# Moving the rows of x and b to every second and every fourth partition in an FFT, expert and GLU kernel

## Chip, cores and metric

The kernel runs on one core of one Trainium2 chip. The metric is the device time of one execution in microseconds (us).

## What is computed

Three layers run one after the other over 8 batches of 3072 tokens of 256 channels. Weights and inputs are random float32.

```
X = np.fft.rfft(x, axis=1)
Y = X * (filt_r + 1j * filt_i)[None, :, :]
y = np.fft.irfft(Y, n=3072, axis=1)              # layer 1: a filter along the sequence
x = y.reshape(B * S, D)
skip = x @ w_skip; e = argmax(x @ w_gate)         # layer 2: one of 8 experts for tokens with skip > 0
x += gate * (relu(x @ w1[e]) @ w2[e])             #          (only for those tokens)
xn = x / rms(x) * rms_g                           # layer 3: a gated linear unit
out = (silu(xn @ w_gate) * (xn @ w_val)) @ w_out
```

## The kernel before

`fft_route` (L159) does layer 1 and the choice of experts. A sequence of 3072 tokens is seen as 96 rows of 32 tokens (N1 = 96, N2 = 32). A product with a 96x96 matrix goes over the 96 rows (stage 1), one with 24 matrices of 128x128 over the 32 columns (stage 2), the filter is applied, the same goes back (stage 3), and a 96x96 product ends it (stage 4). Between the stages the data must change its layout, and that is done through DRAM:

| transfer | line | SBUF partitions | size, transfers per step |
|---|---|---|---|
| x, input to SBUF | L209 | 96 | 384 KB, 2 |
| a_d, stage 1 to DRAM | L404 | 96 | 384 KB, 2 |
| a, DRAM to stage 2 | L370 | 128 | 768 KB, 1 |
| b_d, stage 3 to DRAM | L455 | 128 | 768 KB, 1 |
| b, DRAM to stage 4 | L379 | 96 | 768 KB, 1 |
| y, stage 4 to DRAM | L477 | 96 | 384 KB, 2 |

The work is cut into 32 steps, a quarter (Q = 4) of a batch each. The loop at L655 runs as a pipeline by hand: in step s stage 1 works on quarter s, stages 2 and 3 on quarter s - 5, stage 4 on quarter s - 10, and the routing on quarter s - 11. After step 31 nothing is left for stage 1, and the pipeline drains until step 45. The list `seq` (L677) is the order in which the pieces of a step are written down: `f` is stage 2, `v` stage 3 (its third piece, `vp`, is done at the start of the next step), `u1` stage 1, `u4` stage 4, `qu` the squares of x on ScalarE, `tr`, `logits`, `choose`, `rank`, `place`, `gate` and `sc` the routing. Every engine runs its instructions in that order.

All of these transfers are issued from SyncE (SP). Its queue is in order: a transfer whose semaphore isn't there yet holds back all that stand behind it. The transfers take eight semaphores in turn, so each one also waits until the eighth before it has landed.

- `load_x` (L203) fetches x two steps ahead into six tiles of half a step.
- `load_a2` (L364) stands at the very start of step s and fetches the tile for step s + 1. It reads whole columns, so the first of a batch (s divisible by 4) needs all of stage 1's writes of that batch. The last of these is issued at the end of step s - 1.
- `load_b4` (L374) stands behind `vp` and fetches the tile for stage 4 of step s + 1. The first of a batch (s = 9, 13, 17, ...) needs all four of stage 3's writes of that batch. The last of these is issued by `vp`, right ahead of it.
- Stage 1's matmul (L395) takes its x tile, stage 4's (L471) its b tile, as the moving operand, with the 96x96 constants `d1` and `d4`.

When the pipeline drains, the generator `then` (`moe`, L903) takes the room of the x tiles (`front`) for expert weights and tokens. `glu` (L1523) is the last layer.

Of the kernel before, what the change touches and what calls it, by code (L numbers as in the profile page):

```python
# [10 lines left out]
F32 = mybir.dt.float32  # L11
F16 = mybir.dt.float16
I32 = mybir.dt.int32
U32 = mybir.dt.uint32
ACTF = mybir.ActivationFunctionType
# [5 lines left out]
NB, S, D = 8, 3072, 256  # L21
N1, N2, NG = 96, 32, 24
# [19 lines left out]
def shape_constants():  # L42


    pi2 = 2.0 * np.pi
    n1 = np.arange(N1)
    d1 = np.zeros((N1, 4, NG))
    d4 = np.zeros((4, NG, N1))
    t2 = np.zeros((NG, 4, N2, 2, 2, N2))
    t3 = np.zeros((NG, 2, 2, N2, 4, N2))  # L50
    sgn = np.zeros((2, 2, N2, NG))
    kk = np.zeros((2, 2, N2, NG), np.int64)
    n2 = np.arange(N2)
    k2 = np.arange(N2)
    for g in range(NG):
        for u in range(2):
            q = 2 * g + u
            if q == 0:
                for ri, k1 in ((0, 0), (1, N1 // 2)):
                    d1[:, ri, g] = np.cos(pi2 * n1 * k1 / N1)  # L60
                    d4[ri, g, :] = np.cos(pi2 * n1 * k1 / N1) / S
                k = np.where(k2 < 16, N1 * k2, N1 // 2 + N1 * (k2 - 16))
                th = pi2 * np.outer(n2, k) / S
                for s in range(N2):
                    ri = 0 if s < 16 else 1
                    t2[g, ri, :, 0, u, s] = np.cos(th[:, s])
                    t2[g, ri, :, 1, u, s] = -np.sin(th[:, s])
                    t3[g, 0, u, s, ri, :] = 2 * np.cos(th[:, s])
                    t3[g, 1, u, s, ri, :] = -2 * np.sin(th[:, s])
                t2[g, 0, :, 1, u, 0] = np.cos(np.pi * n2)  # L70
                t3[g, 0, u, 0, 0, :] = 1.0
                t3[g, 1, u, 0, 0, :] = np.cos(np.pi * n2)
                kk[0, u, :, g] = k
                kk[1, u, :, g] = k
                kk[1, u, 0, g] = S // 2
                sgn[0, u, :, g] = -1.0
                sgn[1, u, :, g] = 1.0
                sgn[:, u, 0, g] = 0.0
            else:
                d1[:, 2 * u, g] = np.cos(pi2 * n1 * q / N1)  # L80
                d1[:, 2 * u + 1, g] = -np.sin(pi2 * n1 * q / N1)
                d4[2 * u, g, :] = 2 * np.cos(pi2 * n1 * q / N1) / S
                d4[2 * u + 1, g, :] = -2 * np.sin(pi2 * n1 * q / N1) / S
                k = q + N1 * k2
                th = pi2 * np.outer(n2, k) / S
                t2[g, 2 * u, :, 0, u, :] = np.cos(th)
                t2[g, 2 * u + 1, :, 0, u, :] = np.sin(th)
                t2[g, 2 * u, :, 1, u, :] = -np.sin(th)
                t2[g, 2 * u + 1, :, 1, u, :] = np.cos(th)
                t3[g, 0, u, :, 2 * u, :] = np.cos(th).T  # L90
                t3[g, 1, u, :, 2 * u, :] = -np.sin(th).T
                t3[g, 0, u, :, 2 * u + 1, :] = np.sin(th).T
                t3[g, 1, u, :, 2 * u + 1, :] = np.cos(th).T
                up = k > S // 2
                kk[:, u, :, g] = np.where(up, S - k, k)
                sgn[0, u, :, g] = np.where(up, 1.0, -1.0)
                sgn[1, u, :, g] = np.where(up, -1.0, 1.0)
    f = np.float32

    p = np.arange(128)[:, None]  # L100
    w = np.arange(NB * 24)[None, :]
    n, t = np.divmod(w % 6 * 128 + p, N1)
    tok = w // 24 * S + N2 * t + w // 6 % 4 * 8 + n
    return {
        "c_d1": d1.transpose(0, 2, 1).reshape(N1, N1).astype(f),
        "c_d4": d4.transpose(1, 0, 2).reshape(N1, N1).astype(f),
        "c_t2": t2.reshape(NG, 128, 128).transpose(1, 0, 2).astype(f),
        "c_t3": t3[0].reshape(128, 128).astype(f),
        "c_sgn": sgn.reshape(2, 64, NG).transpose(1, 0, 2).reshape(64, 2 * NG).astype(f),
        "c_tri": (np.arange(128)[:, None] < np.arange(128)[None, :]).astype(np.float16),  # L110
        "c_tok": np.stack([tok, 0 * tok], axis=2).astype(np.int32).reshape(128, 2 * NB * 24),
        "c_pri": np.broadcast_to((NE - np.arange(NE)).astype(f), (128, 6, NE)),
        "c_blk": np.concatenate([
            CAP * np.arange(NE), np.zeros(2 * NE),
            (np.arange(NE)[None, :] < np.arange(NE)[:, None]).ravel(), np.arange(NBLK + 8),
        ]).astype(f)[None, :],
        "c_cap": np.broadcast_to((CAP * np.arange(NE)).astype(f), (128, NE)),
    }, kk.reshape(128, NG)
# [40 lines left out]
def fft_route(tc, x, filr, fili, w9, consts, y_dram, lst, lp, front, shared, then):  # L159
# [13 lines left out]
    with ExitStack() as ctx:  # L173
# [2 lines left out]
            tc.tile_pool(name=name, bufs=bufs, **kw))  # L176
        dp = pool("f_dram", 1, space=DRAM)
        cp = pool("f_const", 1, side="right")
        b4p = pool("f_b4", 2, side="right")
        yp = pool("f_y", 4, side="right")  # L180
        tp = pool("f_t", 2, side="right")
        rp = pool("f_r", 2, side="right")
# [15 lines left out]
            (eng or nc.sync).dma_start(out=t, in_=src)  # L198
            return t

        x_t = {}

        def load_x(s):  # L203
            if s < steps:
                b, q = divmod(s, Q)
                for h in range(2):
                    t = front.tile([N1, HC, D], F32, tag="x", name="x")
                    n = q * CH + h * HC
                    nc.sync.dma_start(  # L209
                        out=t, in_=x[b].rearrange("(p n) c -> p n c", p=N1)[:, n:n + HC, :]  # L210
                    )
                    x_t[s, h] = t

        d1 = const("d1", [N1, N1], F32, consts["c_d1"])
        load_x(0)
        load_x(1)
        t2 = fp.tile([128, NG, 128], F32, name="t2")
# [42 lines left out]
                axis=AX.X, op=ALU.max, apply_absolute_value=True,  # L260
            )

        d4 = cp.tile([N1, N1], F32, name="d4")
        tri = cp.tile([128, 128], F16, name="tri")
        pri = cp.tile([128, RC, NE], F32, name="pri")
        basee = lp.tile([128, NE], F32, name="basee")
# [107 lines left out]
        def load_b4(s):  # L374
            if not 0 <= s < steps:
                return
            b, q = divmod(s, Q)
            t = b4p.tile([N1, CH, D], F32, tag="b4", name="b4")
            nc.sync.dma_start(out=t, in_=b_d[b % 3][:, q * CH:(q + 1) * CH])  # L379
            b4_t[s] = t  # L380

        def stage1(s):

            b, q = divmod(s, Q)
            if q == 0:
                sq_t[b] = rp.tile([N1, 2 * Q], F32, tag="sq", name="sq", bufs=4)
            at = {}

            def part(i):
                h, o = divmod(2 * i, HC)  # L390
                xt = x_t[s, h]
                if o == 0:
                    at[h] = ap.tile([N1, HC, D], F32, tag="a", name="a")
                ps = ps_d.tile([N1, 2 * D], F32, tag="d", name="ps1")
                nc.tensor.matmul(  # L395
                    out=ps, lhsT=d1, rhs=xt[:, o:o + 2, :].rearrange("p n c -> p (n c)"),
                    start=True, stop=True,
                )
                nc.scalar.copy(
                    out=at[h][:, o:o + 2, :].rearrange("p n c -> p (n c)"), in_=ps  # L400
                )
                if o + 2 == HC:
                    n = q * CH + h * HC
                    nc.sync.dma_start(out=a_d[b % 3][:, n:n + HC, :], in_=at[h])  # L404

            def square(h):
                jk = fp.tile([N1, HC, D], F16, tag="jk", name="jk")
                nc.scalar.activation(
                    out=jk, in_=x_t[s, h], func=ACTF.Square,
                    accum_out=sq_t[b][:, 2 * q + h:2 * q + h + 1],  # L410
                )
            return [lambda i=i: part(i) for i in range(CH // 2)], [
# [241 lines left out]
        vp = []  # L654
        for s in range(steps + lagr + 3):  # L655
            s2, s4, sr = s - lag2, s - lag4, s - lagr
            load_a2(s2 + 1)
            if s < Q - 1:
                load_x(s + 2)
            for fn in startup.get(s, []):  # L660
# [4 lines left out]
            if s % Q == 2 and lagr < s < steps + Q:  # L665
# [9 lines left out]

            r1a, r1b = ({}, r1) if steps + 5 < s <= steps + 10 else (r1, {})
            seq = [  # L677
                f[0:1], sc[0:1], vp, [lambda: load_b4(s4 + 1)], fmx[0:1], u1[0:1],
                g(r1, "logits"), [lambda: load_x(s + 2)] if s >= Q - 1 else [], qu[0:1], f[1:2],
                tr[0:1], u1[1:2], g(r1, "choose"), sc[1:3], u4[0:1], v[0:1], fmx[1:2], f[2:3],  # L680
                tr[1:2], u4[1:2], g(r1a, "rank"), qu[1:2], g(r1a, "place"), sc[3:5], u1[2:3],
                tr[2:3], v[1:2], fmx[2:3], g(r1, "gate"), u4[2:3], sc[5:6], tr[3:4], u1[3:4],
                u4[3:4], g(r1b, "rank"), g(r1b, "place"), sq,
            ]
            vp = v[2:3]
# [217 lines left out]
def moe(tc, y_dram, lst, c_blk, w1, w2, wsp, lp, front, shared):  # L903
# [12 lines left out]
        while shared["step"] < n:  # L916
            yield

    wf = [front.tile([128, FE], F32, tag="x", name="m_wf") for _ in range(4)]
    x = front.tile([128, 4, D], F32, tag="x", name="m_x")  # L920
    xs = front.tile([128, 4, 2 * D], F16, tag="x", name="m_xs")
    ws = lp.tile([128, 16], F32, name="m_ws")
    ones = lp.tile([128, 128], F32, name="m_ones")

# [788 lines left out]
def run_all(tc, x, filr, fili, w9, w1, w2, wg, wv, wo, rg, consts, out):  # L1713
    with tc.tile_pool(name="scratch", bufs=1, space=DRAM) as dp:
# [1 line left out]
        lst = dp.tile([NE * CAP + TB, 2], I32, name="lst")  # L1716
        wsp = dp.tile([NE, 128, WROW], F16, name="wsp")
        with tc.tile_pool(name="lists", bufs=1, side="right") as lp, ExitStack() as before:
            front = before.enter_context(tc.tile_pool(name="front", bufs=6))
            mctx = tc.manual_schedule()  # L1720
            mctx.__enter__()
            shared = {"ps_m": before.enter_context(tc.tile_pool(name="ps_m", bufs=1, space=PSUM))}
# [41 lines left out]
```

## Time and profile before

| | us |
|---|---|
| median of 3 runs | 3391.66 (3383.09 to 3394.03) |
| profiled execution, its own time | 3414.32 |
| its span, first to last instruction | 3412.5 |
| TensorE busy | 3196.1 |
| VectorE busy | 2255.2 |
| ScalarE busy | 2259.5 |
| GpSimd busy | 1530.4 |

The profile cuts the span into 40 slices of 85 us. The first seven are the FFT, the next nine are mostly the experts, the rest is the GLU. A digit is the busy share of an engine in tenths. The DMA line is the mean busy share of 16 DMA engines, and the one under it what they moved in GB/s. An engine in this kernel waits only for a semaphore: where it idles, the timeline names in brackets how long and what released it.

### The profile page before, as it was taken

How to read it: one execution, taken by the hardware profiler on the slowest of the kernel's cores; microseconds unless marked ns; L12 is line 12 of the kernel's file. 1: busy time of each engine (PE TensorE's matmuls, PEld its weight loads, DVE VectorE, ACT ScalarE, POOL GpSimd, SP SyncE). 2: the span in 40 equal slices, each digit the busy share in tenths (PEclk: the TensorE clock that was granted, in tenths of full speed). 3: DMA queues.
4: the chain of work that ended last, by engine and by line, in shares of the span. 5: the costliest groups of instructions: out<-in, count | busy, mean ns of one | idle time of the engine just before them, and what ended most of it. 6: DMA issues, size and time to landing. Idle time of an engine off the chain costs nothing.

```text
span 3412.5 us, 60927 instructions
## 1 busy us (share of the span) xinstructions
PE 3196.1 (94%) x21784; PEld 2172.4 (64%) x21784; DVE 2255.2 (66%) x4818; ACT 2259.5 (66%) x4950; POOL 1530.4 (45%) x1546
## 2 busy tenths in 40 slices
PE   7888887688998988999999999999999999999999
PEld 3555554355555655767767777776776776776776
DVE  3777776488998645666666666666666666666664
ACT  5556654566766755676676676777667667667665
POOL 2355566456565643344334334334334433433433
PEclk8999997799999999999999999999999999999999
DMA  9899997355556462212111211211221211121110
GB/s 279 276 262 281 275 276 205 109 160 163 166 166 178 132 180 81 56 45 46 51 45 41 56 42 44 55 37 45 47 50 45 47 50 45 44 53 45 41 37 19
DMA packets 374683, 364.73 MB, mean 107 GB/s; under 512 B 260964, under 2 KB 320372, under 8 KB 370022
## 3 DMA queue, kind: packets, MB, share of 16 engines
q1 hardware_dynamic: 357430, 335.28, 35.0%
q0 software_dynamic: 16944, 25.51, 2.6%
q8 instruction: 173, 2.83, 0.3%
q14 instruction: 136, 1.11, 0.1%
HBM read 157.96 MB, written 133.80 MB: 85 GB/s over the span
## 4 chain that ended last, share of the span: by engine, by line
PE 57%; ACT 3%; DVE 1%; DMA 0%; issue 0%; SPq 0%; DVEq 0%; ACTq 0%
PE psa L1581 21%; PE o L1660 20%; PE psb L1581 16%; ACT gc L1598 1%; DVE vc L1592 1%; ACT jk L772 1%; ACT s L1588 0%; ACT hh L1614 0%; DVE rsq_g L132 0%; ACT ot L1673 0%; ACT u L1588 0%; DMA x<-y 0%; PE m_o L1128 0%; DMA xT<-xs 0%; DVE ss L774 0%
## 5 line engine op out<-in xcount | busy, mean ns | idle before, releaser
L1617 POOL TENSOR_TENSOR hl<-vc,hh 128x384 f16<-128x384 f32 x768 | 699.2, 914 | 1247.5 <-ACT hh L1614 1247.1
L1660 PE MATMUL o<-g_wo,hh 128*128 128x256 f16 x4608 | 878.8, 273 | 0.0
L1660 PEld LDWEIGHTS <-hh 128*128 128x128 f16 x4608 | 450.7, 98 | 296.7
L1660 PE MATMUL o<-g_wo,hl 128*128 128x256 f16 x2304 | 628.0, 273 | 0.0
L1581 PE MATMUL psa<-xT,g_vhi 128*128 128x384 f16 x1488 | 484.2, 326 | 8.2 <-DVE vc L1592 8.2
L1581 PE MATMUL psa<-xT,g_ghi 128*128 128x384 f16 x1488 | 484.2, 326 | 0.5 <-DVE gc L1592 0.3
L1614 ACT CAST hh<-vc 128x384 f16<-128x384 f32 x768 | 394.2, 513 | 13.6 <-DVE vc L1604 13.5
L1604 DVE SCALAR_TENSOR_TENSOR vc<-vc,g_st,gc 128x384 f32<-128x384 f32 x576 | 378.8, 680 | 5.7
L1588 ACT COPY s<-psa 128x384 f32<-128x384 f32 x384 | 182.9, 476 | 297.8 <-PE psa L1581 297.7
L1581 PE MATMUL psb<-xT,g_vhi 128*128 128x384 f16 x1116 | 363.1, 326 | 0.0
L1581 PEld LDWEIGHTS <-g_ghi 128*128 128x128 f16 x2688 | 263.0, 98 | 123.2
L1598 ACT ACTIVATE gc<-gc,g_st 128x384 f32<-128x384 f32 x576 | 338.6, 616 | 0.0
L1581 PE MATMUL psb<-xT,g_ghi 128*128 128x384 f16 x1116 | 332.8, 326 | 0.1
L1581 PEld LDWEIGHTS <-g_vhi 128*128 128x128 f16 x2688 | 262.9, 98 | 102.7
L1110 PE MATMUL psa<-m_xT,m_w 128*128 128x512 f16 (+1 forms) x1344 | 318.4, 377 | 9.8 <-DMA m_xT<-m_xs 8.0
L1128 PE MATMUL m_o<-m_w,m_hh 128*128 128x256 f16 x1740 | 305.6, 277 | 14.0 <-PEq L1331 11.1
L1588 ACT COPY s<-psb 128x384 f32<-128x384 f32 x384 | 183.4, 478 | 202.0 <-PE psb L1581 201.8
L1128 PE MATMUL m_o<-m_w,m_hl 128*128 128x256 f16 x870 | 241.4, 277 | 43.2 <-POOL m_hl L1121 32.5
L1581 PE MATMUL psa<-xT,g_glo 128*128 128x384 f16 x744 | 242.5, 326 | 0.0
L1581 PE MATMUL psa<-xT,g_vlo 128*128 128x384 f16 x744 | 242.5, 326 | 0.0
L1660 PEld LDWEIGHTS <-hl 128*128 128x128 f16 x2304 | 225.4, 98 | 26.0 <-POOL hl L1617 0.2
L1592 DVE TENSOR_TENSOR vc<-psb,s 128x384 f32<-128x384 f32 x192 | 106.6, 555 | 196.8 <-PE psb L1581 194.8
(254 smaller groups left out, 6322.6 us busy)
## 6 DMA issues: line engine op xcount, KB each, us to landing
x<-in_x_dram SPq DMA_DIRECT2D x64, 384.0 KB
a_d<-a SPq DMA_DIRECT2D x64, 384.0 KB
a<-a_d SPq DMA_DIRECT2D x32, 768.0 KB
b_d<-bt SPq DMA_DIRECT2D x32, 768.0 KB
b<-b_d SPq DMA_DIRECT2D x32, 768.0 KB
y<-y SPq DMA_DIRECT2D x64, 384.0 KB
x<-y SPq DMA_DIRECT2D x28, 768.0 KB
out_dram<-ot SPq DMA_DIRECT2D x27, 768.0 KB
```

The source lines that it names most:

```text
L772: ops = [(SQUARES[t], lambda t=t: nc.scalar.activation(out=jk, in_=x[:, t, :], func=ACTF.Square, accum_out=ss[:, t:t + 1])) for t in range(T)]
L1110: nc.tensor.matmul(out=ps, lhsT=w[:, k, fs], rhs=d["xT"][:, o + k, 0:n], start=(j == 0), stop=(j == 5),)
L1128: nc.tensor.matmul(out=o[t // 2][:, t % 2, :], lhsT=h[:, ts_], rhs=w_["w2"][:, f, i, :], start=(f == k == t % 2 == 0), stop=(f == KF - 1 a ...
L1581: nc.tensor.matmul(out=ps, lhsT=w_[m][:, q, k, :], rhs=xT[:, o + k, :], start=(j == 0 and bank == p), stop=(j == 2), skip_group_check=True,)
L1588: nc.scalar.copy(out=z[m, n], in_=z[m, p])
L1592: v.tensor_tensor(out=z[m, n], in0=z[m, p], in1=z[m, b], op=ALU.add)
L1598: nc.scalar.activation(out=z["g", n], in_=src, func=ACTF.Silu, scale=st[:, 20:21])
L1604: v.scalar_tensor_tensor(out=z["v", n], in0=src, scalar=st[:, 21:22], in1=z["g", n], op0=ALU.mult, op1=ALU.mult,)
L1614: nc.scalar.copy(out=part(hh, n), in_=z["v", n])
L1617: nc.gpsimd.tensor_tensor(out=part(hl, n), in0=z["v", n], in1=part(hh, n), op=ALU.subtract)
L1660: nc.tensor.matmul(out=o_t[b][:, t % 2, :], lhsT=h[:, f, ts_], rhs=wo16[:, 2 * q + f, k, :], start=(j == 0 and q == 0 and n == first_of[b] ...
```

## The change

Each tile of x and of b now has 128 partitions and holds a whole step (`x_all` has three of them, `b4_all` two). Rows 0 to 63 lie on partitions 0, 2, 4 to 126, and rows 64 to 95 on partitions 1, 5, 9 to 125; `load_rows` needs two transfers for that, of 512 and 256 KB. The other 32 partitions hold zeros, written once by five memsets at the start. `d1` and `d4` are spread in the same way, and the products run over 128 partitions. x keeps two transfers per step, b has two in place of one. A batch's first load of a moves from the start of the step to behind `load_x`, and a batch's first load of b from behind `vp` to behind the second piece of stage 3. Other loads of a and b keep their places.

```diff
+    def spread(d):
+        out = np.zeros((128, N1))
+        out[0::2] = d[0:64]
+        out[1::4] = d[64:]
+        return out.astype(f)
...
-        "c_d1": d1.transpose(0, 2, 1).reshape(N1, N1).astype(f),
-        "c_d4": d4.transpose(1, 0, 2).reshape(N1, N1).astype(f),
+        "c_d1": spread(d1.transpose(0, 2, 1).reshape(N1, N1)),
+        "c_d4": spread(d4.transpose(1, 0, 2).reshape(N1, N1)),
...
+        def load_rows(t, rows):
+            nc.sync.dma_start(out=t[0:128:2], in_=rows[0:64])
+            nc.sync.dma_start(out=t[1:128:4], in_=rows[64:N1])
+
+        x_all = [t.rearrange("p (n c) -> p n c", c=D) for t in front]
...
-                for h in range(2):
-                    t = front.tile([N1, HC, D], F32, tag="x", name="x")
-                    n = q * CH + h * HC
-                    nc.sync.dma_start(
-                        out=t, in_=x[b].rearrange("(p n) c -> p n c", p=N1)[:, n:n + HC, :]
-                    )
-                    x_t[s, h] = t
-
-        d1 = const("d1", [N1, N1], F32, consts["c_d1"])
+                load_rows(x_all[s % 3], x[b].rearrange("(p n) c -> p n c", p=N1)[
+                    :, q * CH:(q + 1) * CH, :])
+
+        b4_all = [b4p.tile([128, CH, D], F32, name=f"b4{i}") for i in range(2)]
+        for i, t in enumerate(front + b4_all):
+            (nc.vector, nc.gpsimd)[i % 2].memset(t, 0.0)
+        d1 = const("d1", [128, N1], F32, consts["c_d1"])
         load_x(0)
         load_x(1)
...
-            t = b4p.tile([N1, CH, D], F32, tag="b4", name="b4")
-            nc.sync.dma_start(out=t, in_=b_d[b % 3][:, q * CH:(q + 1) * CH])
+            t = b4_all[s % 2]
+            load_rows(t, b_d[b % 3][:, q * CH:(q + 1) * CH])
...
-                jk = fp.tile([N1, HC, D], F16, tag="jk", name="jk")
+                jk = fp.tile([128, HC, D], F16, tag="jk", name="jk")
...
-            load_a2(s2 + 1)
+            la, lb = [lambda: load_a2(s2 + 1)], [lambda: load_b4(s4 + 1)]
+            la0, la1 = ([], la) if (s2 + 1) % Q == 0 else (la, [])
+            lb0, lb1 = ([], lb) if (s4 + 1) % Q == 0 else (lb, [])
+            for fn in la0:
+                fn()
...
-                f[0:1], sc[0:1], vp, [lambda: load_b4(s4 + 1)], fmx[0:1], u1[0:1],
-                g(r1, "logits"), [lambda: load_x(s + 2)] if s >= Q - 1 else [], qu[0:1], f[1:2],
+                f[0:1], sc[0:1], vp, lb0, fmx[0:1], u1[0:1],
+                g(r1, "logits"), [lambda: load_x(s + 2)] if s >= Q - 1 else [], la1, qu[0:1], f[1:2],
...
-                tr[2:3], v[1:2], fmx[2:3], g(r1, "gate"), u4[2:3], sc[5:6], tr[3:4], u1[3:4],
+                tr[2:3], v[1:2], lb1, fmx[2:3], g(r1, "gate"), u4[2:3], sc[5:6], tr[3:4], u1[3:4],
...
-    wf = [front.tile([128, FE], F32, tag="x", name="m_wf") for _ in range(4)]
-    x = front.tile([128, 4, D], F32, tag="x", name="m_x")
-    xs = front.tile([128, 4, 2 * D], F16, tag="x", name="m_xs")
+    room = [front[(4 * NB + i) % 3][:, h * FE:(h + 1) * FE] for i in range(3) for h in range(2)]
+    wf = room[0:4]
+    x = room[4].rearrange("p (t c) -> p t c", t=4)
+    xs = room[5].bitcast(F16).rearrange("p (t c) -> p t c", t=4)
```

How the order moves is seen on SP, whose queue the other engines wait for. This is the queue before, in steps 16 and 17 (`a_d_157` is what stage 1 wrote of batch 3, `b_d_162` what stage 3 wrote of batch 2; step 17 begins at the second load of a):

```order
L370 DMA a_1787<-a_d_157 128x6x256
L455 DMA b_d_162<-bt 128x6x256
L379 DMA b_1819<-b_d_161 96x2048
L209 DMA x<-in_x_dram 96x1024 x2
L404 DMA a_d_158<-a 96x1024
L477 DMA y<-y 96x1024
L404 DMA a_d_158<-a 96x1024
L477 DMA y<-y 96x1024
L370 DMA a_1982<-a_d_157 128x6x256
L455 DMA b_d_162<-bt 128x6x256
L379 DMA b_2013<-b_d_162 96x2048
L209 DMA x<-in_x_dram 96x1024 x2
```

The first row waits for the write of a_d that stands just ahead of it, and the load of `b_2013` for the write right over it. This is step 16 of the changed kernel on SP:

```order
L466 DMA b_d_168<-bt 128x6x256
L211 DMA b_119<-b_d_167 64x2048
L212 DMA b_119<-b_d_167 32x2048
L211 DMA x_66<-in_x_dram 64x2048
L212 DMA x_66<-in_x_dram 32x2048
L382 DMA a_1824<-a_d_163 128x6x256
L415 DMA a_d_164<-a 96x1024
L488 DMA y<-y 96x1024
L415 DMA a_d_164<-a 96x1024
L488 DMA y<-y 96x1024
```

The batch's first load of a has moved from the head of the step to behind five other transfers. And this is step 17 of the changed kernel, again on SP:

```order
L382 DMA a_1954<-a_d_163 128x6x256
L466 DMA b_d_168<-bt 128x6x256
L211 DMA x_67<-in_x_dram 64x2048
L212 DMA x_67<-in_x_dram 32x2048
L415 DMA a_d_164<-a 96x1024
L488 DMA y<-y 96x1024
L211 DMA b_118<-b_d_168 64x2048
L212 DMA b_118<-b_d_168 32x2048
L415 DMA a_d_164<-a 96x1024
L488 DMA y<-y 96x1024
```

Four transfers now stand between the write of b_d and the first load that needs it. On TensorE the order of the matmuls is what it was, step by step.

## Rows read from the trace of the kernel before

**Rows 1.** The page's 40 slices of the span: TensorE, DMA share and GB/s.

```profile
PE   7888887688998988999999999999999999999999
...
DMA  9899997355556462212111211211221211121110
GB/s 279 276 262 281 275 276 205 109 160 163 166 166 178 132 180 81 56 45 46 51 45 41 56 42 44 55 37 45 47 50 45 47 50 45 44 53 45 41 37 19
```

**Rows 2.** Windows: us, engines' busy time (instructions), granted clock, DMA share, GB/s.

```profile
core 0: us, PE busy (x) PEld busy (x) DVE busy (x) ACT busy (x) POOL busy (x), PEclk, DMA share, GB/s
159.00:498.00 339.00, 298.07 (x1705) 184.35 (x1701) 243.79 (x643) 202.84 (x404) 189.72 (x177) 0.96 0.93 274
...
1600.00:3412.00 1812.00, 1797.15 (x12975) 1268.72 (x12972) 1147.95 (x2158) 1264.75 (x2880) 720.87 (x773) 1.00 0.18 45
```

**Rows 3.** TensorE's timeline: first logits matmul of steps 13, 18, 19, 20, 32, 34, 35.

```profile
158.70 0.20 PE L545 MATMUL lg<-w9s,yh 128*128 128x18 f16 x2
...
247.10 0.20 PE L545 MATMUL lg<-w9s,yh 128*128 128x18 f16 x2
...
267.40 0.20 PE L545 MATMUL lg<-w9s,yh 128*128 128x18 f16 x2
...
282.27 0.20 PE L545 MATMUL lg<-w9s,yh 128*128 128x18 f16 x2
...
491.30 0.20 PE L545 MATMUL lg<-w9s,yh 128*128 128x18 f16 x2
...
517.43 0.20 PE L545 MATMUL lg<-w9s,yh 128*128 128x18 f16 x2
...
535.48 0.20 PE L545 MATMUL lg<-w9s,yh 128*128 128x18 f16 x2
```

**Rows 4.** SP's waits, 0 to 580 us: line, releaser, us in total, times, longest.

```profile
SPq L379 <- DMA b_d<-bt: 83.0, 8, 13.4
SPq L370 <- DMA a_d<-a: 46.4, 7, 11.7
```

**Rows 5.** SP's timeline, steps 15 to 17: start, us, line, transfer.

```profile
213.42 0.30 SPq L404 DMA_DIRECT2D a_d<-a  x1
...
222.67 0.38 SPq L370 DMA_DIRECT2D a<-a_d  x1
...
234.88 0.38 SPq L455 DMA_DIRECT2D b_d<-bt  x1
247.90 0.32 SPq L379 DMA_DIRECT2D b<-b_d  x1
```

**Rows 6.** TensorE's timeline, step 18: the wait for b.

```profile
253.85 1.07 PE L471 MATMUL ps<-b,d 96*96 96x512 f32 x2 [3.84 <-DMA b<-b_d]
```

**Rows 7.** Windows: step 16's transfers, the pause behind them, and TensorE after b's wait.

```profile
226.00:230.00 4.00, 3.22 (x13) 1.65 (x12) 2.20 (x9) 2.29 (x5) 3.20 (x4) 1.00 1.09 375
230.00:236.00 6.00, 5.38 (x43) 3.19 (x42) 4.73 (x8) 3.58 (x7) 2.74 (x3) 1.00 1.03 250
236.00:240.00 4.00, 4.00 (x26) 2.59 (x25) 3.77 (x12) 2.78 (x6) 2.77 (x3) 1.00 1.11 377
246.00:248.00 2.00, 2.00 (x29) 1.30 (x29) 1.72 (x3) 1.28 (x4) 0.08 (x1) 1.00 0.00 1
...
254.00:258.00 4.00, 4.00 (x11) 2.74 (x11) 0.00 (x0) 1.17 (x2) 0.90 (x1) 0.63 1.02 349
```

**Rows 8.** Windows of the start: x alone (96 partitions); filters fr and fi (64 partitions).

```profile
5.00:11.00 6.00, 5.41 (x8) 1.73 (x8) 0.00 (x0) 3.30 (x7) 0.00 (x0) 1.00 1.03 266
42.00:46.00 4.00, 4.00 (x9) 2.32 (x9) 2.71 (x4) 1.06 (x2) 0.53 (x1) 0.50 1.00 204
```

**Rows 9.** Timeline of the first 6 us: x's transfers and TensorE's first wait.

```profile
1.21 2.97 SPq L209 DMA_DIRECT2D x<-in_x_dram  x6
...
5.59 5.47 PE L395 MATMUL ps<-x,d 96*96 96x512 f32 x8 [5.59 <-DMA x<-in_x_dram]
```

**Rows 10.** Memsets by source and by line: ns or busy us, mean ns.

```profile
L998 POOL MEMSET m_x<- x1: 945/945/945, 514.0 to 514.0; 128x1024 f32 x1
...
L294 DVE MEMSET ones<- 128x128 f32 x1 | 0.2, 165 | 0.8 <-PEq L1753 0.8
```

More of the change, by code (lines that the diff above doesn't have):

```diff
@@ L178, in fft_route @@
         cp = pool("f_const", 1, side="right")
-        b4p = pool("f_b4", 2, side="right")
+        b4p = pool("f_b4", 1, side="right")
         yp = pool("f_y", 4, side="right")
@@ L199, in const @@
             return t
-        x_t = {}
+        def load_rows(t, rows):
+            nc.sync.dma_start(out=t[0:128:2], in_=rows[0:64])
+            nc.sync.dma_start(out=t[1:128:4], in_=rows[64:N1])
+        x_all = [t.rearrange("p (n c) -> p n c", c=D) for t in front]
         def load_x(s):
@@ L261, in filter_max @@
             )
-        d4 = cp.tile([N1, N1], F32, name="d4")
+        d4 = cp.tile([128, N1], F32, name="d4")
         tri = cp.tile([128, 128], F16, name="tri")
@@ L385, in stage1 @@
             if q == 0:
-                sq_t[b] = rp.tile([N1, 2 * Q], F32, tag="sq", name="sq", bufs=4)
+                sq_t[b] = rp.tile([128, 2 * Q], F32, tag="sq", name="sq", bufs=4)
             at = {}
@@ L390, in part @@
                 h, o = divmod(2 * i, HC)
-                xt = x_t[s, h]
                 if o == 0:
@@ L395, in part @@
                 nc.tensor.matmul(
-                    out=ps, lhsT=d1, rhs=xt[:, o:o + 2, :].rearrange("p n c -> p (n c)"),
+                    out=ps, lhsT=d1, rhs=x_all[s % 3][:, 2 * i:2 * i + 2, :].rearrange("p n c -> p (n c)"),
                     start=True, stop=True,
@@ L406, in square @@
             def square(h):
-                jk = fp.tile([N1, HC, D], F16, tag="jk", name="jk")
+                jk = fp.tile([128, HC, D], F16, tag="jk", name="jk")
                 nc.scalar.activation(
-                    out=jk, in_=x_t[s, h], func=ACTF.Square,
+                    out=jk, in_=x_all[s % 3][:, h * HC:(h + 1) * HC, :], func=ACTF.Square,
                     accum_out=sq_t[b][:, 2 * q + h:2 * q + h + 1],
@@ L1718, in run_all @@
         with tc.tile_pool(name="lists", bufs=1, side="right") as lp, ExitStack() as before:
-            front = before.enter_context(tc.tile_pool(name="front", bufs=6))
+            fp = before.enter_context(tc.tile_pool(name="front", bufs=1))
+            front = [fp.tile([128, 8 * D], F32, name=f"x{i}") for i in range(3)]
             mctx = tc.manual_schedule()
```

## The prediction

> **What bounds the kernel now.** I read the 40 slices first [rows 1]. The DMA digit is 9 or 8 in the first six slices, where 262 to 281 GB/s move, and falls to 2 or 1 in the second half, where TensorE shows 9 throughout. The GLU has no room for this change: TensorE is busy for 1797.15 of 1812.00 us there [rows 2]. All that the change touches lies in the FFT, roughly the first 570 us. In its steady part, 159 to 498 us, TensorE is busy for 298.07 of 339.00 us, at a mean granted clock of 0.96, while the DMA engines show a share of 0.93 and 274 GB/s [rows 2]. Two resources are nearly full there, and neither is quite full.
>
> The step's length tells which holds. From the first logits matmul of step 19 to that of step 20 it is 282.27 - 267.40 = 14.87 us [rows 3], and TensorE waits for nothing in it: this is its work. But step 13 to step 32 takes 491.30 - 158.70 = 332.6 us, 17.5 us for each of 19 steps [rows 3]. The excess over TensorE's work is 332.6 - 19 x 14.87 = 50.1 us. That is the most that this stretch can give.
>
> Where the excess sits is seen in SP's waits [rows 4]: eight waits of L379 for the write of b_d, 83.0 us, and seven of L370 for the write of a_d, 46.4 us, both once per batch. The timeline shows one of each [rows 5]. The last a_d write is issued at 213.42, and the load of a behind it only at 222.67; the b_d write at 234.88, the load of b at 247.90. For 9 and 13 us SP issues nothing, the transfers in flight run out (1 GB/s from 246 to 248 us [rows 7]), and the next load starts on an empty queue. [...] Step 18, with this wait, lasts 267.40 - 247.10 = 20.3 us [rows 3], 5.4 us too long.
>
> Why is the wait so long? Because the write stands behind a backlog. Bytes against time sort the transfers [rows 7]. From 226 to 230 us, 375 GB/s: 1.5 MB, the a load and the b_d write (two times 0.79 MB). From 230 to 236 us, 250 GB/s: 1.5 MB, the b load and both x loads. From 236 to 240 us, 377 GB/s: two writes of a_d and two of y. That reading is a sorting by size and order. Per step it makes 1.57 MB / 375 + 1.57 MB / 250 + 1.57 MB / 377 = 4.2 + 6.3 + 4.2 = 14.7 us of transfer for 14.87 us of TensorE work. With no slack, a stop of a few us is never caught up.
>
> **The parts of the change.**
>
> *Spreading x and b.* The slow third is the loads to 96 partitions. At the start x alone moves at 266 GB/s [rows 8], and the filter parts for 64 partitions at 204 GB/s, at a DMA share of 1.00 [rows 8]; the 128-partition pair reaches 375. So the rate rises with the span of partitions that a transfer covers. After the change each transfer spans all 128, with 64 or 32 rows. No row shows such a pattern. The low end takes the rate by the count of rows: 204 GB/s for 64, half of it for 32. The high end is 375 GB/s by the span. I take the high end, since the stores from 96 partitions, with no more rows, run at 377 [rows 7]: the count of rows alone does not set the rate. x and b then need 4.2 us in place of 6.3, and a step's transfers 12.6 us, 2.3 us below TensorE's work.
>
> [...]
>
> *Moving the first loads.* The a_d write has five transfers behind it before the load of a asks for it, the b_d write four before the load of b. SP still waits, but the engines have some 2 MB to move meanwhile. Queued behind the waiting load of a are that step's a_d and y writes, which nobody needs within the step; behind the load of b the second a_d and y writes. The loads must land by the next step's first stage 2 (a) and first stage 4 (b). b is the tighter: issued past the middle of step 17, it has about 0.8 of a step, 12 us, against 253.85 - 247.90 = 6 us from issue to use now [rows 5, 6].
>
> *Step sum, steps 13 to 31.* Five of the eight waits for b fall here, 5 x 5.4 = 27 us; I give back 85%, 23 us. The other 23 us of the excess (a's waits, backlog) I give back by somewhat under a half, 10 us. Together **33 us**, with 0 and 50 as ends. The step would average 15.8 us.
>
> *Filling, steps 4 to 12.* The transfers are the bound there too [rows 1]. Some eight x loads and three b loads are each 1.05 us shorter (half of 6.3 - 4.2), 11.6 us in all; I take two thirds, **8 us**, with ends 0 and 15.
>
> *Draining.* Step 34 lasts 535.48 - 517.43 = 18.05 us [rows 3] and holds the same stop; **4 us**, ends 0 and 8.
>
> *Start.* Before, x's first transfer is issued at 1.21 us and TensorE starts at 5.59 [rows 9]. Now x waits for a memset of 128x2048. GpSimd's of half that size took 945 ns [rows 10], VectorE's 128x128 took 165 ns [rows 10], so each costs between 1.9 us (twice the one) and 2.6 us (16 times the other). And the first matmul needs 768 KB in place of 384. I take **-2 us**, ends 0 and -4.
>
> *The rest at nothing.* The matmuls' columns are unchanged, 128 rows in place of 96 add none. The squares of x read 128 partitions in the same number of columns. The 37 further transfers cost SP 0.3 to 0.4 us each [rows 5], while it waits for most of a step anyway; without that cover it would be 15 us. The expert part keeps its order.
>
> The sum is 33 + 8 + 4 - 2 = 43 us. The profiled execution, 3414.3 us (span 3412.5), would come to 3371; it lies 22.7 us above the median of the runs shown, and the same 43 us off the median, 3391.7, gives **3349 us**.
>
> **The rivals.**
>
> *Only the order helps (0.15).* The spread loads stay at 250 GB/s. Transfers then need 14.7 us per step against 14.87, the stops go but nothing is ever caught up. For it: 64 rows at 204 GB/s. I give 21 us for the steps, 2 for the filling, 3 for the drain, less 2: 24 us, **3368 us**.
>
> *The moved load of b comes too late (0.12).* If b's write has not landed by the middle of its step, SP stands still with two writes behind it, and TensorE waits for b as now. The 23 us stay; what is left is 10 + 8 - 2 = 16 us, **3376 us**. For it: the write took 13 us from 234.88 to 247.90. Against: it stood behind a backlog that faster loads shorten.
>
> *The split makes the loads slower (0.07).* If the rate follows the rows of each transfer, a tile takes 0.52 MB / 204 + 0.26 MB / 102 = 5.1 us, x and b 10.3 in place of 6.3, a step's transfers 18.7 us. Every step then lasts at least that: 19 x (18.7 - 17.5) = 23 us, 11 x (5.1 - 3.15) = 21 in filling, 2 at the start, **3438 us**. [...]
>
> *It is given back (0.06).* The FFT ends earlier, but the experts' first tokens or weights wait for something else, or the second transfer of a pair waits for the first after all: within 10 us of **3392 us**.
>
> **How the numbers follow.** The forecast has 0.60, with its own range from 3328 (all of 50 + 8 + 8 - 2 = 64 us) to 3362. The range to 3386 takes in the first two rivals and leaves out the last two and a little at the fast end. A run of this kernel can tell some 0.3%, 10 us, from no change. Faster by more: 0.60 + 0.15 + 0.10 = 0.85; within: 0.08; slower: 0.07.
>
> **What would show it.** Right: intervals of 15 to 16 us between the logits matmuls, no window near 0 GB/s at a batch's turn, L471's waits for b gone, x alone at the start well above 266 GB/s, a lower DMA share at a higher rate per busy engine. Wrong: x alone at or below 266 GB/s; waits for b of 3 us in every fourth step; steps of 17 us and more; or steps of 15 us and an end that did not move.

## The result, and the profile after

| | before | after |
|---|---|---|
| median, us | 3391.39 (4 runs, 3383.09 to 3394.03) | 3356.26 (4 runs, 3352.03 to 3358.74) |
| ratio, 95% interval | | 0.9902 (0.9889 to 0.9915) |
| profiled execution, its own time | 3414.32 | 3352.03 |
| its span | 3412.5 | 3350.2 |

The changed kernel is 35 us faster, with 43 forecast and 3349 in place of 3356. The profiled execution of after is the fastest of its four, that of before lay 22.9 us above its median, so the two spans differ by 62.3 us. A second profile of before (the first experiment) has a span of 3390.3, 40.1 us above after, and is the better partner.

The page's slices of after answer to [rows 1]:

```profile
PE   6899997889889889999999999999999999999999
...
DMA  8899985465555462121112112111111211211110
GB/s 262 294 297 328 317 282 173 132 184 164 168 162 155 136 166 58 42 57 36 46 47 51 46 42 57 37 46 47 51 46 42 57 36 46 47 51 46 42 38 20
```

TensorE shows 9 in four slices of the FFT, and the DMA engines move up to 328 GB/s where 281 was the most. The windows of after are the steady part (step 13 to 32), two of the start, a gap in the drain and the GLU, with the columns of [rows 2]:

```profile
171.69:454.38 282.69, 275.33 (x1664) 172.34 (x1663) 235.56 (x627) 195.52 (x398) 184.91 (x171) 1.00 0.95 309
...
6.00:9.00 3.00, 1.06 (x2) 0.52 (x3) 1.64 (x5) 0.00 (x0) 0.00 (x0) 1.00 0.97 328
9.00:11.00 2.00, 2.00 (x4) 0.70 (x3) 0.00 (x0) 1.03 (x2) 0.00 (x0) 1.00 0.94 389
...
530.00:540.00 10.00, 0.00 (x0) 0.00 (x0) 2.21 (x11) 0.81 (x2) 7.56 (x9) 0.62 0.57 160
1600.00:3350.00 1750.00, 1735.42 (x12529) 1225.03 (x12526) 1109.34 (x2082) 1219.84 (x2777) 698.59 (x748) 1.00 0.18 45
```

x alone at the start moves at 328 and 389 GB/s in these two windows, 352 over both, in place of 266 [rows 8]. In the steady part TensorE is busy for 275.33 of 282.69 us at a mean granted clock of 1.00 in place of 0.96 [rows 2], with 309 GB/s beside it in place of 274. The first logits matmul of steps 13, 19, 20, 32, 38 and 39 in after, for [rows 3]:

```profile
171.69 0.20 PE L556 MATMUL lg<-w9s,yh 128*128 128x18 f16 x2
...
262.24 0.20 PE L556 MATMUL lg<-w9s,yh 128*128 128x18 f16 x2
...
277.13 0.20 PE L556 MATMUL lg<-w9s,yh 128*128 128x18 f16 x2
...
454.38 0.20 PE L556 MATMUL lg<-w9s,yh 128*128 128x18 f16 x2
...
528.13 0.20 PE L556 MATMUL lg<-w9s,yh 128*128 128x18 f16 x2
...
548.41 0.20 PE L556 MATMUL lg<-w9s,yh 128*128 128x18 f16 x2
```

Step 13 to 32 takes 282.7 us, 19 x 14.88: the whole excess of 50 us is gone. (The 14.87 us of step 19 in the forecast hold one wait of 0.36 us for VectorE, which was overlooked and changes little.) But step 13 begins 13 us **later** than before (171.69 against 158.70), and step 38 lasts 20.3 us. SP's waits up to 580 us, for [rows 4]:

```profile
SPq L488 <- ACT y L485: 134.3, 58, 7.9
...
SPq L961 <- DMA lst<-dat,pos: 10.4, 1, 10.4
...
SPq L212 <- DMA b_d<-bt: 3.5, 1, 3.5
```

The eight waits for b_d and seven for a_d have become one of 3.5 us. SP waits for ScalarE's copies instead, which means for the work itself. One wait of 10.4 us is for the scatters into `lst`. Here is where TensorE of after waits long for a load, in steps 5, 13 and 38:

```profile
48.86 2.08 PE L437 MATMUL ps<-a,t 128*128 128x256 f32 x4 [8.73 <-DMA a<-a_d]
...
167.39 2.07 PE L437 MATMUL ps<-a,t 128*128 128x256 f32 x4 [5.80 <-DMA a<-a_d]
...
541.43 1.99 PE L482 MATMUL ps<-b,d 128*96 128x512 f32 x2 [11.48 <-DMA b<-b_d]
```

The same two places of steps 5 and 13 on TensorE's timeline of the kernel before:

```profile
41.12 2.07 PE L426 MATMUL ps<-a,t 128*128 128x256 f32 x4 [2.93 <-DMA a<-a_d]
...
156.00 1.13 PE L426 MATMUL ps<-a,t 128*128 128x256 f32 x4 [1.38 <-DMA a<-a_d]
```

SP's timeline of after shows what stands ahead of each of the three loads (start, us, line, transfer):

```profile
35.02 0.42 SPq L240 DMA_DIRECT2D t<-in_c_t_dram  x1
35.50 0.70 SPq L241 DMA_DIRECT2D fr<-in_filr_dram  x1
36.24 0.62 SPq L242 DMA_DIRECT2D fi<-in_fili_dram  x1
36.96 0.54 SPq L211 DMA_DIRECT2D x<-in_x_dram  x1
37.55 0.59 SPq L212 DMA_DIRECT2D x<-in_x_dram  x1
38.25 0.60 SPq L382 DMA_DIRECT2D a<-a_d  x1
...
148.43 5.19 SPq L296 DMA_DIRECT2D lst<-pre  x7
...
155.14 0.50 SPq L211 DMA_DIRECT2D b<-b_d  x1
...
157.11 0.59 SPq L211 DMA_DIRECT2D x<-in_x_dram  x1
...
158.42 0.58 SPq L382 DMA_DIRECT2D a<-a_d  x1
...
521.89 0.38 SPq L466 DMA_DIRECT2D b_d<-bt  x1
532.75 0.83 SPq L961 DMA_DIRECT2D m_ids<-lst  x2
...
534.23 0.46 SPq L211 DMA_DIRECT2D b<-b_d  x1
```

In step 4 the load of a stands behind three constants of the second filter group and an x tile; in step 12 behind eight writes that fill the lists, a write of b_d, b and x; in step 37 the load of b behind the fetch of `m_ids`, which waits for the scatters. Against both profiles of before, by stages (the first logits matmul of steps 13, 32 and 42, the first expert matmul, TensorE's first load of `g_vhi` as weights, which starts the GLU here, and the span):

| stretch | first before | second before | after | gain | forecast |
|---|---|---|---|---|---|
| start to step 13 | 158.7 | 158.6 | 171.7 | -13 | +6 |
| step 13 to 32 | 332.6 | 337.1 | 282.7 | 50 to 54 | +33 |
| step 32 to 42 | 137.5 | 124.9 | 122.4 | 2 to 15 | +4 |
| step 42 to the first expert matmul | 6.3 | 5.5 | 5.7 | 0 to 1 | 0 |
| experts | 684.4 | 671.5 | 675.8 | -4 to 9 | 0 |
| GLU | 2093.0 | 2092.8 | 2091.9 | 1 | 0 |

The 22 us that the first profile of before has over the second lie in the drain and the experts, where two executions of one kernel differ by 13 us each; nothing is read from that here.

### The profile page after: what moved, and what is told of

Same layout as the page of the kernel before. It is cut to its first block, busy times and chain, and to the rows that moved or that the text cites. A ratio compares the mean times of both kernels' runs of the same rounds, so it can differ in the third digit from the quotient of the medians.

```text
span 3350.2 us, 60920 instructions
## 1 busy us (share of the span) xinstructions
PE 3169.7 (95%) x21784; PEld 2158.5 (64%) x21784; DVE 2261.3 (67%) x4821; ACT 2252.3 (67%) x4950; POOL 1534.4 (46%) x1548
## 4 chain that ended last, share of the span: by engine, by line
PE 58%; ACT 3%; DVE 1%; DMA 0%; issue 0%; POOL 0%; SPq 0%; DVEq 0%; ACTq 0%
PE psa L1599 21%; PE o L1678 21%; PE psb L1599 16%; ACT gc L1616 1%; ACT jk L788 1%; DVE vc L1610 1%; ACT s L1606 0%; ACT hh L1632 0%; DVE rsq_g L141 0%; ACT ot L1691 0%; ACT u L1606 0%; PE m_o L1146 0%; DMA xT<-xs 0%; DMA x<-y 0%; DVE ss L790 0%
## 5 line engine op out<-in xcount | busy, mean ns | idle before, releaser
L1128 PE MATMUL psa<-m_xT,m_w 128*128 128x512 f16 (+1 forms) x1344 | 320.2, 379 | 10.5 <-DMA m_xT<-x 8.7
```

Source lines behind the costliest of these rows:

```text
L1128: nc.tensor.matmul(out=ps, lhsT=w[:, k, fs], rhs=d["xT"][:, o + k, 0:n], start=(j == 0), stop=(j == 5),)
```

## The experiments

Each is timed beside the kernel before on the same chip; where its median is another than 3391, it is named. "Steps" is the time from the first logits matmul of step 13 to that of step 32.

**Before, once more.**

> The kernel before, profiled once more. The profiled execution that the prediction was made from took 3414.3 us, 22.7 us above the median of its runs; where that time lay is not known. If it lay in the FFT, this execution's steps 13 to 32 are shorter than 332.6 us (about 310); if it lay behind it, they are 330 us again and the end of the FFT stays near 629 us.

3392.1 us, steps 337.1 us, so the 22 us more of the first profile do not lie in the steps. SP's waits in this second profile of before:

```profile
SPq L379 <- DMA b_d<-bt: 86.7, 8, 13.9
SPq L370 <- DMA a_d<-a: 58.7, 10, 10.3
```

The stops of [rows 4] are a property of the kernel, not of one execution.

**Spreading without the order.**

```diff
-            la0, la1 = ([], la) if (s2 + 1) % Q == 0 else (la, [])
-            lb0, lb1 = ([], lb) if (s4 + 1) % Q == 0 else (lb, [])
+            la0, la1 = la, []
+            lb0, lb1 = lb, []
```

> The changed kernel with both first loads put back to their old places. Theory (spreading gives the slack, the order takes care of the stops, both are needed): SP's stops return, but without backlog they last 4 to 6 us in place of 10 to 13; steps 13 to 32 take 290 to 300 us in place of 282.7, and the filling is some 12 us shorter than in the changed kernel, since the batch's first load of a no longer stands behind the filters and the list's writes: 3350 to 3360 us in all, about the change's time. Rival (the order does it, spreading nothing): 3380 us or more, stops of 10 us and more.

3365.97 us beside 3394.22, ratio 0.9909 (0.9891 to 0.9927). Steps 309.6 us, step 13 at 157.3. The first logits matmul of steps 13 and 32, and SP's waits:

```profile
157.30 0.20 PE L556 MATMUL lg<-w9s,yh 128*128 128x18 f16 x2
...
466.94 0.20 PE L556 MATMUL lg<-w9s,yh 128*128 128x18 f16 x2
```

```profile
SPq L212 <- DMA b_d<-bt: 54.3, 8, 8.3
SPq L488 <- DMA b_d<-bt: 43.8, 13, 5.5
SPq L382 <- DMA a_d<-a: 42.4, 13, 6.5
```

The longest stop falls from 13.9 to 8.3 us, which fits a backlog that is shorter in time (that cause is argued, not measured). But the stops stay, and 27 us of the excess with them, more than I expected to be left. Over the whole kernel, though, the ratio of spreading alone cannot be told from the changed kernel's 0.9902 (0.9889 to 0.9915).

**The order without spreading.** The kernel before with the two moved loads, and its b in one transfer as ever.

```diff
-            load_a2(s2 + 1)
+            la, lb = [lambda: load_a2(s2 + 1)], [lambda: load_b4(s4 + 1)]
+            la0, la1 = ([], la) if (s2 + 1) % Q == 0 else (la, [])
+            lb0, lb1 = ([], lb) if (s4 + 1) % Q == 0 else (lb, [])
+            for fn in la0:
+                fn()
...
-                f[0:1], sc[0:1], vp, [lambda: load_b4(s4 + 1)], fmx[0:1], u1[0:1],
-                g(r1, "logits"), [lambda: load_x(s + 2)] if s >= Q - 1 else [], qu[0:1], f[1:2],
+                f[0:1], sc[0:1], vp, lb0, fmx[0:1], u1[0:1],
+                g(r1, "logits"), [lambda: load_x(s + 2)] if s >= Q - 1 else [], la1, qu[0:1], f[1:2],
...
-                tr[2:3], v[1:2], fmx[2:3], g(r1, "gate"), u4[2:3], sc[5:6], tr[3:4], u1[3:4],
+                tr[2:3], v[1:2], lb1, fmx[2:3], g(r1, "gate"), u4[2:3], sc[5:6], tr[3:4], u1[3:4],
```

> The kernel before with only the two first loads moved, x and b on 96 partitions in the old transfers. Theory: transfers of 14.7 us a step against 14.87 us of TensorE work leave no slack; steps 13 to 32 take 295 to 310 us, the filling loses some 10 us as in the changed kernel, 3370 to 3390 us in all. Rival (the order alone suffices): steps 13 to 32 take 285 us, as in the change, and the time is within 5 us of its 3356 us.

3400.26 us beside 3394.22, ratio 1.0016 (1.0005 to 1.0028): no gain, and slower than either theory had it. The window of the steps (320.2 us) and, below it, one of TensorE's waits for a batch's first a:

```profile
176.02:496.20 320.18, 283.54 (x1664) 177.14 (x1663) 235.69 (x627) 195.66 (x398) 184.25 (x171) 0.95 0.98 272
```

```profile
449.20 1.22 PE L426 MATMUL ps<-a,t 128*128 128x256 f32 x2 [10.98 <-DMA a<-a_d]
```

SP's waits for a_d fall to 11.7 us and for b_d to 4.2, the DMA share rises to 0.98, and the rate stays at 272 GB/s. At that share a load that is issued later only lands later: TensorE waits 6 to 11 us for the first a of each of the four batches that begin in this window. Step 13 starts at 176.0, 17 us late, which eats what the steps win.

**Only b late, only a late.** The line of the other load is put back as in the second experiment.

> The changed kernel with the batch's first load of a at its old place, the head of the step; only b's first load is late. Theory (b's stop is the costly one, since it falls behind the larger backlog; a's move costs the filling 10 us and gives 1 to 2 us per batch later): waits for a_d on SP of 4 to 6 us come back, steps 13 to 32 take some 290 us, step 13 begins near 156 us, 3350 to 3357 us in all, no slower than the change. Rival (a's move pays as much as b's): 3365 us and more.

> The changed kernel with the batch's first load of b at its old place, right behind the write that it needs; only a's first load is late. Theory: the filling is as long as in the changed kernel (step 13 near 170 us), each batch has a stop for b_d of 6 to 8 us on SP and a wait of 1 to 2 us at TensorE; 3365 to 3375 us. Rival (the stop for b costs nothing once the loads are spread): 3356 us.

Beside 3422.12 us: b late 3378.48, ratio 0.9881 (0.9862 to 0.9900), steps 301.8, step 13 at 156.3. a late 3388.56, ratio 0.9908 (0.9884 to 0.9931), steps 289.2, step 13 at 173.4, and no long wait for b in the drain. So the late a makes step 13 late, the late b makes the drain's wait, and in the steps a's move is worth more than b's: from 309.6 us it gives 20, b's 8, both 27. I had expected b's stop to be the costly one. Over the whole kernel neither of the two can be told from spreading alone, nor from both.

**a late only where the pipeline is full.**

```diff
-            la0, la1 = ([], la) if (s2 + 1) % Q == 0 else (la, [])
+            la0, la1 = ([], la) if (s2 + 1) % Q == 0 and s >= 16 else (la, [])
```

> The changed kernel, but in steps 4, 8 and 12 the batch's first load of a stands at the head of the step again, ahead of the filters and the list's writes. Theory (the filling lost 8.7 and 5.8 us at TensorE to that load): the waits at steps 5 and 13 fall to 3 and 1 us, step 13 begins near 160 us in place of 171.7, and the time is 8 to 12 us below the changed kernel, 3345 us. Rival (the filling is bound by the sum of its transfers): the wait moves to another load and the time stays at 3356 us.

3350.76 us beside 3394.22, ratio 0.9862 (0.9844 to 0.9881), against 0.9902 (0.9889 to 0.9915) for the changed kernel, and 15.2 us below spreading alone, which was timed beside the same 3394.22 and has 0.9909 (0.9891 to 0.9927). So the moved loads do pay over the whole kernel, once a's move is kept out of the filling. TensorE's waits for a in steps 5 and 13, and the window of the steps:

```profile
41.77 1.13 PE L437 MATMUL ps<-a,t 128*128 128x256 f32 x4 [2.98 <-DMA a<-a_d]
...
169.04 1.13 PE L437 MATMUL ps<-a,t 128*128 128x256 f32 x4 [1.17 <-DMA a<-a_d]
```

```profile
155.97:445.47 289.50, 275.82 (x1664) 172.27 (x1663) 236.36 (x628) 196.15 (x398) 184.83 (x171) 1.00 0.98 312
```

The two waits fall from 8.73 and 5.80 us to 2.98 and 1.17. Step 13 starts at 156.0, 15.7 us earlier than in after, so a's place was the whole delay. The first expert matmul starts at 577.9 us, in after at 582.5: in these two profiles 11 of the 15.7 us are lost on the way. Steps take 289.5 us (step 14 alone 18.4, with a wait of 2.95 us for ScalarE), and step 38 21.9, with a wait of 13.25 us for b behind a wait of 10.6 us for the scatters.

**Rows packed, in the same two transfers.** As the changed kernel, with rows 0 to 95 on partitions 0 to 95.

```diff
-        out[0::2] = d[0:64]
-        out[1::4] = d[64:]
+        out[0:96] = d
...
-            nc.sync.dma_start(out=t[0:128:2], in_=rows[0:64])
-            nc.sync.dma_start(out=t[1:128:4], in_=rows[64:N1])
+            nc.sync.dma_start(out=t[0:64], in_=rows[0:64])
+            nc.sync.dma_start(out=t[64:N1], in_=rows[64:N1])
```

> The changed kernel with the rows back on partitions 0 to 95: the same two transfers of 64 and 32 rows with 8 KB each, the same memsets, constants and order, only the partitions differ. Theory (where the rows lie sets the rate): x alone at the start moves at 250 to 290 GB/s as before, not at 330 to 390; the first loads of a wait 5 to 10 us at TensorE in every batch as with the order alone; 3395 to 3405 us. Rival (the longer rows of 8 KB, or the larger and smaller transfer, make the loads faster): 3356 us, and x alone above 320 GB/s.

3428.02 us beside 3422.12, ratio 1.0011 (0.9996 to 1.0026). The start with x alone:

```profile
6.00:9.00 3.00, 0.00 (x0) 0.00 (x0) 1.64 (x5) 0.00 (x0) 0.00 (x0) 1.00 1.03 238
9.00:11.00 2.00, 1.62 (x2) 0.68 (x3) 0.00 (x0) 0.00 (x0) 0.00 (x0) 1.00 0.95 209
```

Over both windows that is 226 GB/s, where after has 352 in the same windows. Everything but the partitions is as in after, and the gain is gone. x moves even more slowly than the 250 to 290 GB/s that I had expected. The place of the rows is what pays: not the larger rows, not the split, not the order.

**Rows in two halves.** 48 rows on partitions 0 to 47 and 48 on 64 to 111.

```diff
-        out[0::2] = d[0:64]
-        out[1::4] = d[64:]
+        out[0:48] = d[0:48]
+        out[64:112] = d[48:]
...
-            nc.sync.dma_start(out=t[0:128:2], in_=rows[0:64])
-            nc.sync.dma_start(out=t[1:128:4], in_=rows[64:N1])
+            nc.sync.dma_start(out=t[0:48], in_=rows[0:48])
+            nc.sync.dma_start(out=t[64:112], in_=rows[48:N1])
```

> The changed kernel with rows 0 to 47 on partitions 0 to 47 and rows 48 to 95 on partitions 64 to 111, two transfers of 384 KB. [...] Theory B (only the balance between the lower and the upper 64 partitions counts, or the span covered): both halves hold 48 rows, so x alone at 340 GB/s or more and about 3356 us.

3445.66 us beside 3422.12, ratio 1.0075 (1.0057 to 1.0093): slower than packed. x alone:

```profile
6.00:9.00 3.00, 0.00 (x0) 0.00 (x0) 1.64 (x5) 0.00 (x0) 0.00 (x0) 1.00 1.01 186
9.00:11.00 2.00, 1.00 (x2) 0.46 (x3) 0.00 (x0) 0.00 (x0) 0.00 (x0) 1.00 1.01 180
```

Over both windows that is 184 GB/s, the slowest of the patterns at the start, and far below the 340 GB/s or more of theory B. An even count of rows in the two halves does not help here, with a transfer for each half: 96 partitions in one transfer moved at 266 GB/s [rows 8]. In the steps the halves and the packed rows take the same, 329.4 and 329.0 us. The halves lose against packed before step 13, which starts at 192.2 us in place of 181.8.

**The drain, the filling, the start.** Beside 3413.5 us: b's first load of step 37 early again; this with a late from step 16 on; and this with the first memset cut in two.

```diff
-            lb0, lb1 = ([], lb) if (s4 + 1) % Q == 0 else (lb, [])
+            lb0, lb1 = ([], lb) if (s4 + 1) % Q == 0 and s < 36 else (lb, [])
...
-            (nc.vector, nc.gpsimd)[i % 2].memset(t, 0.0)
+            if i == 0:
+                nc.vector.memset(t[:, 0:HC * D], 0.0)
+                nc.gpsimd.memset(t[:, HC * D:], 0.0)
+            else:
+                (nc.vector, nc.gpsimd)[i % 2].memset(t, 0.0)
```

> The changed kernel, with the first load of b in step 37 back behind vp, ahead of the fetch of m_ids. Theory (the moved load of b costs the drain, since it stands behind the fetch of m_ids, which waits for the scatters): TensorE's wait for b of 11.5 us in step 38 goes, the time from the first logits matmul of step 38 to that of step 40 falls from 28.3 us to some 24, and the end moves by 3 to 5 us: ratio to before 0.989, 3352. Rival (the drain waits for the scatters anyway, and the experts' first tokens set the end): steps 38 to 40 shorter, the end within 1 us of the changed kernel's, ratio 0.990.

> Both at once: a's first load of a batch late only from step 16 on, b's late except in step 37. If the two costs are separate they add: 5.5 us (filling, as measured alone) plus 3 to 5 (drain), ratio 0.985, some 3347. If the drain starts earlier but the scatters it waits for don't, the part of the filling is lost at the m_ids fetch and the ratio stays at 0.986 to 0.987.

> As e10, and the memset of x's first tile is cut in two halves, one on VectorE and one on GpSimd. Theory (the start's 2.4 us are the memset ahead of x's first transfer plus the larger first tile): x's first transfer is issued at 2.1 to 2.3 us instead of 3.03, TensorE starts at 7.0 to 7.2 instead of 7.94, and of the 0.8 us the end gets all or nothing: too little to measure. Rival (the start waits for the transfer's bytes, behind d1): TensorE's start stays at 7.9.

Drain alone: 3377.10 us, ratio 0.9892 (0.9874 to 0.9910), not to be told from the change's 0.9902. Both: 3367.18, 0.9867 (0.9848 to 0.9886), not to be told from 0.9862 with the filling's edit alone. With the memset: 3363.15, 0.9854 (0.9834 to 0.9874); x's first transfer is issued at 2.02 us and TensorE starts at 6.83, 1.1 us earlier than in after, too little to show at the end.

TensorE's wait for b in step 38 is gone in all three, and the gain of 3 to 5 us that I expected from it is not found. With the edit alone, steps 38 and 39 last 30.6 us, after 28.3 in the changed kernel, and step 38 still takes 19.2. But the same two steps last 37.1 and 24.2 us in the two profiles of before, so no single pair of profiles can settle this. The fetch of `m_ids` is issued at 534.3 us, against 532.8. This is step 40 of the kernel with both edits:

```profile
535.00:556.00 21.00, 12.09 (x41) 5.20 (x42) 8.24 (x28) 7.70 (x14) 14.09 (x14) 0.50 0.49 157
```

It lasts 20.8 us, at a granted clock of 0.50. TensorE, VectorE and ScalarE all stand still for much of it, and the trace names no releaser for most of TensorE's gaps. So this execution has a stall in step 40 instead. What holds the engines there stays open. From step 36 to 42 the drain takes 62.3 us with both edits, 68.8 with the filling's alone, 67.4 in after and 73.8 with the drain's alone. In the two profiles of before it takes 78.3 and 63.6, so these differences lie within what two executions of one kernel show, and nothing is read from them.

## Why the prediction was right, point by point

**The bound: right.** The two nearly full resources, the excess of 50 us and the batch's stops as its place are what the runs show. With x and b spread and the first loads moved, the steps fall to 14.88 us.

**The rate: right, and it carries the rest.** I took 375 GB/s for the spread loads, and x alone measured 328 and 389, 352 over both windows. I had no reason but "the stores run at 377 with no more rows", and the packed kernel shows that the choice was between gain and no gain: that it came out is in part luck. The slow rival (rates by rows, 3438 us, 1.4% above the kernel before) is refuted for this pattern. The halves, another pattern, go half that way, to 1.0075. The rival of the order is refuted twice: order alone gives 1.0016, spreading alone 0.9909.

What it is in the place of the rows that sets the rate is not shown. The order of the loads' rates over the start agrees with my reading of [rows 8], that the rate rises with the span of partitions that a transfer covers: 352 GB/s where each transfer of a tile spans nearly all 128, 266 for 96 in one transfer, 226 for 64 and 32, 184 for 48 and 48. That is an order in four cases and not a cause, it gives no size, and the stores from 96 partitions at 377 [rows 7] do not fit it.

**"Moving the first loads": right for the steps, wrong outside them.** SP's stops are gone and b's waits in the steps too. I called b the tighter; in the steps TensorE has no wait for b left and four for a, 3.7 us in all, and a's move is worth 20 us there against b's 8.

**"Step sum, steps 13 to 31", 33 us: mis-sized.** It measured 50 to 54, its upper end. Giving back "85%" of b's waits and "somewhat under a half" of the rest was too little, because no rest stayed. The 5.4 us taken for each wait for b are step 18's length over 14.87 us [rows 3]; in that step TensorE waits 3.84 us for b [rows 6], and the granted clock over 254 to 258 us is 0.63 [rows 7].

**"Filling, steps 4 to 12", 8 us: this step failed.** It measured -13 us together with the start. The forecast counted shorter loads and left out that the moved load of a stands behind other things there: in step 4 behind three constants and x, in step 12 behind eight list writes, b and x. The part on the moved loads names a_d and y behind the load, and five transfers before it in step 16, but I never read the order in the filling, where TensorE of after waits 8.73 and 5.80 us for a. With a early in the filling, step 13 starts at 156.0 us. That is only 2.6 to 2.7 us earlier than in the two profiles of before; with the start's 2.4 us added back, the shorter loads gave some 5 of the 8 us.

**"Draining", 4 us: unsettled.** Its gain is 2 or 15 us, by the profile of before that is taken. The wait of 11.48 us for b behind `m_ids` has the effect of the rival "The moved load of b comes too late", in one step, though the scatters make it and not b's own write. Removing that wait gave no gain that could be measured.

**"Start", -2 us: right.** x's first transfer is issued at 3.03 us and TensorE starts at 7.94, against 5.59 [rows 9], so 2.4 us are lost. The memset is 1.8 us by GpSimd and 1.76 by VectorE, under my bounds of 1.9 and 2.6:

```profile
0.73 1.80 POOL L225 MEMSET x<- 128x2048 f32 x1 [0.29 <-POOLq L1772]
1.24 1.76 DVE L225 MEMSET x<- 128x2048 f32 x1 [1.24 <-PEq L1772]
3.03 0.60 SPq L211 DMA_DIRECT2D x<-in_x_dram  x1
...
7.94 1.99 PE L406 MATMUL ps<-x,d 128*96 128x512 f32 x2 [7.94 <-DMA x<-in_x_dram]
```

**"The rest at nothing": held as far as the runs can tell.** The GLU differs by 1 us. In the steps a matmul of stage 1 takes 600 ns over 128 partitions in after and 602 over 96 before, and the squares of x 1066 and 1059 ns. The further transfers are 32 and not 37, b's alone.

So two errors cancelled: 17 to 21 us too little in the steps, 19 too much in the filling and start. The sum of 43 was nearer than its terms by luck.

## What to carry to other kernels

A tile that has fewer rows than partitions is worth spreading over all of them when its load is on a DMA queue as full as this one (a share of 0.93 in the steps [rows 2]): here the same 96 rows moved at 352 GB/s in place of 266 at the start, for memsets once and a constant with zero rows. A load that waits for a write belongs behind independent transfers, but only where its consumer has time: read the queue's order in the filling and the drain too, since a move that saves a stop in the steady part can cost much of that at the ends (here 27 us saved in the steps, and step 13 begins 15.7 us later). Moving a wait behind a full queue gained nothing here (1.0016, at a DMA share of 0.98 in the steps); make the transfers shorter first.

## What was not expected of the hardware

Two transfers of 48 rows, one in each half of the partitions, move x at 180 to 186 GB/s, slower than 64 and 32 rows packed (209 to 238), and both slower than 96 partitions in one transfer (264 to 266 in the second profile of before). So splitting the rows costs rate here, and only the spread wins it back. The split tiles also have rows of 8 KB in place of 4, and no run has the one without the other.
